# How the first batch's inputs are loaded: chunk by chunk over SyncE and GpSimd, with a new order of all instructions

## The chip, the cores and the metric

The kernel runs on one core of one Trainium2 chip. The metric is the device time of one execution in microseconds (us). Engines are named as the profile names them: PE is TensorE, PEld its weight loads, DVE VectorE, ACT ScalarE, POOL GpSimd, SP SyncE. SP computes nothing here: it issues DMAs on the hardware queue q1. DMAs issued by POOL go to the software queue q0.

## The reference

Two stages, cut to what is computed. Shapes: B, H, S, D = 4, 8, 768, 48, and d_model = H*D = 384.

```python
mag = np.sqrt(a_re * a_re + a_im * a_im)
scale = np.minimum(mag, 0.999) / (mag + 1e-06)
a_re_n, a_im_n = (a_re * scale, a_im * scale)
for t in range(S):
    ar, ai = a_re_n[:, :, t, :, None], a_im_n[:, :, t, :, None]
    S_re, S_im = ar * S_re - ai * S_im + kv(t), ar * S_im + ai * S_re
    y[:, :, t] = q[:, :, t] @ S_re
...
xn = (x - mean) / sqrt(var + 1e-6) * g_ln
out = x + np.maximum(xn @ w_ch1, 0.0) @ w_ch2
```

`kv(t)` is the outer product of k and v at time t. The first stage is a recurrence over time with a complex gate a; `x` is its output with the heads put side by side. All inputs and the output are float32.

## The kernel before, in words

The 768 time steps of each batch are cut into 6 chunks of 128 (24 chunks in all, g = 0 to 23). The chunks stand in groups G0 to G8 (the list `phases`): G0 is chunk 0, G1 chunks 1 and 2, G2 chunks 3 to 5, all of batch 0; G3 is chunks 6 to 8, and so on by threes. G0 and G1 share the first phase.

For each group, `gate_exp` works out the decay of the gate: `ln` of a_re (L411) and its exponential (L414) on ACT, `r` = a_im times that (L393, DVE or POOL by `HOW['r']`), the square of r (`r2`, L393 on DVE or POOL, L397 on ACT), ln(1 + r2) on ACT (L424), their sum and cap on DVE (L427, L434), a cumulative sum over the chunk as a matmul with `u_half` (L440), and two exponentials of it (L445, tile `epn`). A small DMA on SP, `edge`, carries the last row of `epn` (L449). `gate_trig` then needs ACT's other table: arctan of r (L495), sums carried from chunk to chunk (`carry`, L508), the phase by matmuls with `u_turn` (L532 to L536), sine and cosine on ACT (L546) with DVE's passes L543 and L549, the products of q and k with `epn` (`qk`, L584) and of these with sine and cosine (`stk`, L590). ACT's tables are swapped at L372, twice in a phase.

For each chunk, `attention` transposes q and k into `qt` and `kt` (matmuls L617, copies L626; for the later chunks a DMA transpose on SP), forms scores (L642), masks them on DVE (L646), multiplies by v (L668, L670), and carries the state (L711, L713, L718). `feed` is the second stage: moments of x (L734 or L739), its transpose (L750, L754), the first matmul with the folded weight `w1c` (L780), ReLU on ACT or DVE (L786, L788), the second matmul (L801), the residual (L805) and the store on SP (L809). `w1c` is folded at the start from `w1r` and the gains (L310, L320, L324).

Every instruction is added to a plan, and the list `HOW['order']` says in which order they are written out; an engine runs its own in that order and waits where an operand is missing. The strings of `HOW` say which engine takes each operation (V, A, P for DVE, ACT, POOL). `HOW['fill']` gives lengths of filler matmuls on PE ahead of some operations (L169, L173); their results are overwritten.

`HOW['loads']` lists the loads as (what, first, end, engine). "a" is a_re and a_im, "s" is q, k and v; "g", "w1", "w2" are the gains and the thirds of the two weights. a stays float32, the others become bfloat16 on the way. Of batch 0 each array is one tile with all 6 chunks, and `load_fn` has three forms: all six chunks (L213), one chunk (L215), and two chunks that lie three apart (L217, `STEP`): ('a', 1, 3, 'P') loads chunks 1 and 4. By the order, SP issues before its first edge: a_re 0, a_re 3, a_im 0; then edge G0, a_im 3, edge G1. POOL issues: w1 0, a_im 1+4, a_re 1+4, a_re 2+5, a_im 2+5, the gains, (u_half), k 2+5, k 1+4, w1 1, q 0+3, k 0+3, (ident), q 2+5, (u_turn), q 1+4, w1 2, v 1+4, (q of G0, k of G1), v 0+3, (q of G1, k of G0), w2 0, w2 1, (cosine stack of G0), v 2+5, a_re of batch 1, (mask), w2 2, a_im of batch 1, and so on. What stands in brackets is not a load but POOL's work between them: the constants, and the products L584 and L590.

Of the kernel before, what the change touches and what calls it, by code (L numbers as in the profile page):

```python
# [24 lines left out]
STEP = 3  # L25
HOW = {'loads': [('a', 0, 1, 'Y'), ('a', 3, 4, 'Y'), ('a', 1, 3, 'P'), ('a', 2, 4, 'P'), ('g', 0, 0, 'P'),
           ('w1', 0, 0, 'P'), ('w1', 1, 0, 'P'), ('w1', 2, 0, 'P'), ('s', 0, 2, 'P'), ('s', 1, 3, 'P'),
           ('s', 2, 4, 'P'), ('w2', 0, 0, 'P'), ('w2', 1, 0, 'P'), ('w2', 2, 0, 'P'), ('a', 6, 12, 'P'),
# [7 lines left out]
 'r2': 'AVVVVAAAAVVVVVVVVVVVVVVV',  # L36
 'r': 'VVVVVVVVVVPVPPPPPPVPPPPP',
 'carry': 'VVVVPVVVVVPVVVVVPVVVVVPV',
 'st': 'AVVVVVAA',
 'x': 'AAAAAAAVAVVAVAAAVAAAAAAA',  # L40
 'edge': 'YYYYYYYYYYYYYYYYYYYYYYYY',
 'cos': 'VVVVVVVVVVVVVVVVVVVVVVVV',
 'qt': 'AVVVAVVVAVVAAAAAAAAAAAAA',
 'kt': 'AAVAAVVAVVVAVVVVVVVVVVVV',
 'relu': 'AAVVAAAAAAAAAAAVVVAAVAAAAAAVAAVAAAVAAAAVAVAVAVVV',
 'qk': 'PPPPVVPVPVVVVVPPVVVVVVVVVVVVVVVVVVVVVVVVVVVVVVVV',
 'stk': 'VPVVVVVVVVVVVVVVPVVVVVVVVVVVVVVVVVVVVVVVVVVVVVVV',
 'at': 'VVVVVVVVVVVVVVVVVVVVVVVV',
 'xc': 'VAVAAVVAVAVAVVVVVVVVVVVV',
 'xt': 'PPPPPPPPPPPPDDDDDDDDDDDD',  # L50
 'qkt': 'PPPPPPPPPPPPDDDDDDDDDDDD',
 'order': [11, 12, 34, 191, 16, 9, 23, 20, 14, 26, 29, 32, 0, 61, 52, 36, 40, 192, 193, 204, 205, 43, 1, 58, 194, 2,
           206, 195, 207, 196, 208, 4, 209, 178, 49, 197, 198, 210, 199, 38, 201, 200, 211, 55, 212, 202, 183, 213,
           18, 223, 179, 185, 214, 215, 5, 184, 217, 235, 8, 7, 181, 218, 182, 46, 227, 6, 219, 228, 220, 10, 234,
           230, 221, 231, 224, 222, 232, 67, 225, 187, 233, 69, 186, 238, 226, 493, 188, 189, 239, 180, 64, 464, 236,
           240, 470, 190, 465, 243, 241, 73, 242, 244, 471, 237, 245, 3, 487, 71, 246, 462, 488, 485, 80, 463, 510,
           247, 494, 486, 251, 508, 252, 511, 248, 253, 472, 509, 249, 466, 473, 250, 254, 467, 489, 256, 495, 490,
           468, 512, 257, 496, 491, 229, 469, 516, 258, 513, 492, 259, 260, 474, 475, 271, 498, 497, 87, 264, 476,
           514, 261, 499, 479, 515, 265, 502, 518, 267, 520, 263, 477, 266, 262, 521, 503, 480, 522, 268, 478, 94,
           270, 269, 524, 272, 538, 500, 274, 519, 539, 273, 481, 275, 517, 101, 276, 501, 530, 532, 525, 279, 523,  # L60
           504, 278, 277, 533, 280, 531, 281, 555, 482, 553, 534, 505, 556, 526, 282, 506, 554, 283, 535, 284, 576,
           285, 574, 577, 287, 286, 536, 575, 288, 557, 527, 289, 540, 302, 558, 528, 578, 292, 290, 541, 483, 293,
           579, 561, 559, 537, 298, 294, 562, 543, 299, 295, 542, 544, 560, 300, 580, 296, 303, 564, 136, 545, 565,
           297, 581, 304, 584, 301, 547, 108, 566, 306, 305, 602, 548, 603, 563, 594, 307, 596, 595, 604, 585, 617,
           546, 597, 619, 618, 638, 308, 598, 605, 588, 620, 599, 310, 568, 639, 122, 309, 621, 311, 549, 567, 312,
           622, 313, 600, 586, 601, 314, 589, 569, 625, 115, 587, 640, 315, 582, 319, 623, 321, 641, 316, 320, 626,
           607, 317, 642, 583, 624, 570, 318, 608, 322, 324, 335, 643, 609, 325, 550, 627, 326, 327, 551, 610, 606,
           628, 334, 328, 644, 571, 330, 629, 329, 572, 590, 331, 645, 332, 129, 336, 333, 630, 338, 337, 650, 164,
           646, 339, 660, 647, 591, 683, 340, 661, 611, 592, 684, 662, 612, 342, 685, 663, 356, 632, 686, 343, 668,
           664, 631, 648, 613, 341, 633, 357, 669, 651, 665, 344, 358, 687, 670, 688, 359, 345, 704, 666, 652, 671,  # L70
           360, 705, 667, 143, 346, 361, 691, 706, 362, 347, 653, 348, 649, 634, 707, 363, 349, 150, 350, 708, 364,
           614, 673, 365, 674, 709, 654, 367, 689, 366, 655, 368, 635, 370, 351, 656, 353, 672, 352, 690, 369, 354,
           384, 373, 615, 694, 675, 695, 383, 374, 657, 696, 676, 658, 375, 636, 396, 371, 387, 376, 692, 697, 388,
           377, 379, 378, 710, 380, 711, 381, 389, 385, 382, 730, 714, 698, 715, 386, 392, 390, 677, 391, 724, 732,
           678, 393, 790, 731, 716, 733, 699, 791, 394, 745, 712, 395, 718, 397, 751, 400, 679, 398, 764, 401, 399,
           726, 402, 700, 727, 784, 719, 752, 717, 403, 728, 747, 729, 418, 720, 693, 735, 748, 713, 419, 805, 766,
           404, 749, 767, 750, 405, 770, 754, 680, 786, 771, 420, 406, 768, 787, 824, 737, 422, 769, 407, 701, 792,
           421, 774, 793, 807, 738, 788, 157, 408, 681, 423, 756, 702, 409, 789, 808, 811, 757, 795, 739, 721, 826,
           424, 410, 827, 758, 411, 809, 425, 776, 412, 740, 426, 413, 777, 778, 810, 772, 814, 415, 427, 794, 741,
           446, 428, 734, 429, 759, 414, 812, 430, 797, 416, 431, 171, 432, 722, 435, 459, 760, 458, 436, 753, 798,  # L80
           773, 816, 779, 449, 437, 445, 742, 438, 817, 761, 762, 441, 439, 828, 442, 799, 440, 450, 829, 818, 832,
           443, 454, 447, 444, 451, 743, 780, 448, 452, 455, 800, 842, 456, 460, 813, 850, 834, 781, 453, 782, 863,
           848, 836, 849, 457, 851, 801, 830, 819, 835, 837, 882, 831, 844, 461, 820, 845, 433, 869, 902, 821, 846,
           865, 870, 847, 838, 866, 853, 802, 884, 923, 867, 885, 888, 868, 871, 889, 886, 872, 908, 904, 887, 909,
           910, 905, 852, 822, 855, 892, 911, 906, 839, 803, 856, 857, 840, 929, 907, 925, 858, 913, 874, 926, 890,
           942, 891, 896, 927, 897, 859, 928, 912, 875, 876, 860, 931, 894, 861, 877, 932, 930, 915, 895, 944, 916,
           878, 945, 917, 879, 936, 918, 946, 937, 898, 947, 948, 950, 949, 919, 880, 934, 920, 899, 921, 900, 952,
           935, 954, 953, 938, 955, 956, 939, 940, 957, 958],
 'fill': {187: 0.92, 199: 3.58, 219: 1.07, 464: 0.59, 487: 2.58}}


class Plan:

    PIPE = {"V": 0.08, "A": 0.09}

    def __init__(self, rings, slots):
        self.ops, self.makers, self.touch = [], {}, {}
        self.rings, self.slots = rings, slots  # L100
# [24 lines left out]
def kernel(  # L125
# [15 lines left out]
    NCH = S // C  # L141
# [78 lines left out]
    def issue(eng, us, makes, fn, a, pieces, each, got, after=(), hog=False):  # L220
        key = ("dma", len(plan.ops))
        plan.add(ENG[eng], us, (fn, a), [], [key] + makes)
        for i in range(pieces):
            plan.add("Q", each, None, [key], [("moved", len(plan.ops))] + (got if i == pieces - 1 else []),
                     lag=2.0, ring=ENG[eng])

    def load(eng, g0, g1, names, after=()):

        b, c0, c1 = g0 // NCH, g0 % NCH, g0 % NCH + g1 - g0
        us = 0.5 if eng is Y else 0.66 + 0.26 * (c1 - c0)  # L230
        for n in names:
# [642 lines left out]
```

## Time and profile before

| | us |
|---|---|
| median of 3 runs (213.97 to 214.59) | 214.07 |
| the profiled execution, its own time | 214.43 |
| its span, first to last instruction | 212.6 |
| PE busy | 173.3 |
| PEld busy | 135.6 |
| DVE busy | 164.8 |
| ACT busy | 146.3 |
| POOL busy | 102.8 |

The span is the time of the profiled execution without what lies ahead of its first and behind its last instruction. Busy times of engines overlap, so no one of them is the time; what counts is which engine the others wait for in each stretch. Rows of the timeline give the start, the time, the engine, the line, the operation, its output and input, and in square brackets how long the engine stood idle before and what ended that. A row that joins several instructions says how many (x2). DMA rows name the queue, its packets and megabytes in the window asked for, and their time as a share of the 16 DMA engines' time.

### The profile page before, as it was taken

The numbers are of one execution on the slowest core, as the hardware profiler recorded it, in microseconds if no ns is written. First come the engines' busy times: TensorE is split into PE (matmuls) and PEld (weight loads), VectorE is DVE, ScalarE is ACT, GpSimd is POOL, SyncE is SP. The second block draws the span as 40 slices with busy tenths as digits, with TensorE's granted clock in tenths as the row PEclk, the third lists the DMA queues.
The fourth block names the chain that finished last, engine by engine and source line by source line (L and its number), as shares of the span: only waits on it lengthen the run. The fifth ranks groups of instructions, "written<-read, shape, count | busy, mean of one in ns | idle before, by whom it ended". The sixth has DMA issues, their size and how long they took to land.

```text
span 212.6 us, 5419 instructions
## 1 busy us (share of the span) xinstructions
PE 173.3 (82%) x2296; PEld 135.6 (64%) x2296; DVE 164.8 (78%) x262; ACT 146.3 (69%) x205; POOL 102.8 (48%) x89
## 2 busy tenths in 40 slices
PE   0019744979999899998978989987999996999992
PEld 0003314968977688776765857676776765988770
DVE  1018799999999999979899999987987994554351
ACT  4025947499998999988997978967898514453210
POOL 8986798708541476196994010293285820010100
PEclk9999995799999999999999999999999998799999
DMA  6999999994999299999999928969969797752122
GB/s 97 238 184 160 162 134 171 222 240 71 144 119 109 74 75 210 158 161 190 162 71 232 225 92 161 232 144 171 172 65 154 169 192 170 198 120 59 56 77 76
DMA packets 116997, 31.44 MB, mean 148 GB/s; under 512 B 109100, under 2 KB 114956, under 8 KB 116972
## 3 DMA queue, kind: packets, MB, share of 16 engines
q0 software_dynamic: 79104, 18.09, 92.6%
q1 hardware_dynamic: 37868, 13.00, 26.5%
q8 instruction: 18, 0.29, 0.6%
q14 instruction: 7, 0.06, 0.1%
HBM read 28.31 MB, written 4.72 MB: 155 GB/s over the span
## 4 chain that ended last, share of the span: by engine, by line
PE 40%; DVE 22%; DMA 12%; issue 9%; ACT 8%; POOL 5%; SPq 1%; DVEq 0%; POOLq 0%; ACTq 0%
PE h_ps L780 13%; PE o_ps L801 13%; DMA qkt<-stk 8%; DMA ar<-in_a_re_dram 5%; DVE stk L590 4%; PE a_ps L642 3%; DVE w1c L324 3%; PE qk_ps L169 2%; DVE lm L427 2%; ACT epn L445 2%; DVE w L549 2%; PE qk_ps L617 1%; ACT ht L786 1%; DVE o L805 1%; PE l_ps L440 1%
## 5 line engine op out<-in xcount | busy, mean ns | idle before, releaser
L780 PE MATMUL h_ps<-xt,w1c 128*128 128x128 bf16 x864 | 54.6, 221 | 0.2
L780 PEld LDWEIGHTS <-w1c 128*128 128x128 bf16 x864 | 50.7, 99 | 2.4 <-issue 0.6
L801 PE MATMUL o_ps<-w2b,ht 128*128 128x384 bf16 x288 | 50.4, 326 | 0.0
L801 PEld LDWEIGHTS <-ht 128*128 128x128 bf16 x288 | 27.3, 98 | 17.0 <-issue 0.4
L646 DVE TENSOR_TENSOR at<-a_ps,mask 128x1024 bf16<-128x1024 f32 x24 | 29.3, 1219 | 10.0 <-PE a_ps L642 9.7
L786 ACT ACTIVATE ht<-h_ps 128x1024 bf16<-128x1024 f32 (+1 forms) x33 | 26.7, 825 | 11.2 <-PE h_ps L780 11.2
L584 POOL TENSOR_TENSOR epn<-qk,epn 128x1152 bf16<-128x1152 bf16 (+2 forms) x8 | 14.6, 1828 | 17.7 <-ACT epn L445 15.1
L744 POOL TENSOR_SCALAR rs<-mv 128x3 f32<-128x3 f32 x8 | 2.2, 278 | 40.8 <-ACT junk L734 26.2
L445 ACT ACTIVATE epn<-l_ps 128x384 bf16<-128x384 f32 (+1 forms) x32 | 18.6, 652 | 4.7 <-PE l_ps L440 4.6
L805 DVE SCALAR_TENSOR_TENSOR o<-o_ps,rs,x 128x384 f32<-128x384 f32 x24 | 14.4, 610 | 9.5 <-PE o_ps L801 6.5
L642 PE MATMUL a_ps<-qkt 128*128 128x128 bf16 x192 | 15.1, 223 | 3.9 <-DMA qkt<-stk 2.9
L173 PE MATMUL l_ps<-ident 128*128 128x512 bf16 x16 | 5.7, 532 | 15.0 <-POOL ident masks.py:199 15.0
L411 ACT ACTIVATE rec<-ar 128x1152 f32<-128x1152 f32 (+2 forms) x9 | 9.5, 1054 | 11.6 <-DMA ar<-in_a_re_dram 11.6
L393 DVE TENSOR_TENSOR r<-ai,m 128x384 bf16<-128x384 f32 x12 | 6.2, 560 | 14.0 <-DMA ai<-in_a_im_dram 10.9
L372 ACT ACT_TABLE_LOAD x12 | 15.4, 1283 | 0.9 <-PEq L858 0.7
L173 PEld LDWEIGHTS <-ident 128*128 128x128 bf16 x24 | 2.8, 118 | 20.7 <-POOL ident masks.py:199 15.0
L642 PEld LDWEIGHTS <-qkt 128*128 128x128 bf16 x192 | 12.0, 99 | 5.4 <-DMA qkt<-stk 3.2
L788 DVE TENSOR_SCALAR ht<-h_ps 128x512 bf16<-128x512 f32 (+1 forms) x15 | 13.2, 891 | 2.5 <-PE h_ps L780 2.4
L617 PE MATMUL qk_ps<-ident,stk 128*128 128x128 bf16 x192 | 13.6, 223 | 1.6 <-DVE stk L590 1.3
L617 PEld LDWEIGHTS <-stk 128*128 128x128 bf16 x192 | 11.9, 99 | 2.5 <-DVE stk L590 1.5
L424 ACT ACTIVATE m<-lm,one 128x1152 f32<-128x1152 bf16 (+2 forms) x9 | 10.3, 1149 | 4.1 <-DVE lm L393 4.0
L393 POOL TENSOR_TENSOR r<-ai,m 128x384 bf16<-128x384 f32 x12 | 11.6, 994 | 2.9 <-ACT m L414 2.8
(106 smaller groups left out, 388.4 us busy)
## 6 DMA issues: line engine op xcount, KB each, us to landing
out_dram<-o SPq DMA_DIRECT2D x24, 192.0 KB, 3.9
ar<-in_a_re_dram POOLq DMA_DIRECT2D x3, 1152.0 KB, 10.3
ai<-in_a_im_dram POOLq DMA_DIRECT2D x3, 1152.0 KB, 12.0
qk<-in_q_dram POOLq DMA_DIRECT2D x3, 576.0 KB, 9.9
qk<-in_k_dram POOLq DMA_DIRECT2D x3, 576.0 KB, 9.9
v<-in_v_dram POOLq DMA_DIRECT2D x3, 576.0 KB, 8.4
w1r<-in_moe_w_ch_dram POOLq DMA_DIRECT2D x3, 384.0 KB, 10.3
w2b<-in_moe_w_ch_dram POOLq DMA_DIRECT2D x3, 384.0 KB, 7.2
```

The costliest lines, as they stand in the source:

```text
L372: op(A, 1.28, old, [key], lambda: A.preload_act_table_set(TABLES[which]))
L393: times = lambda eng, out, x, y: eng.tensor_tensor(out=out, in0=x, in1=y, op=ALU.mult)
L445: A.activation(out=o, in_=banks(G["l_ps", j], m), func=AF.Exp, scale=(1.0, -1.0)[s])
L584: eng.tensor_tensor(out=o, in0=part(G, "qk"[s]).rearrange("p h c d -> p c h d"), in1=i, op=ALU.mult)
L617: T.transpose(ps[:, h], G["stk"][:, int(which == "ks"), j, ts(h, C)], K["ident"])
L642: T.matmul(ch["a"][:, h], lhsT=ch["kt"][:, h], rhs=ch["qt"][:, h], start=True, stop=True)
L646: V.tensor_tensor(out=ch["at"], in0=ch["a"], in1=K["mask"].unsqueeze(1).to_broadcast([C, H, C]), op=ALU.mult)
L780: T.matmul(ps[:, jj], lhsT=w1c[:, i, ts(j0 + jj, C)], rhs=ch["xt"][:, i], start=(i == 0), stop=(i == ND - 1))
L786: A.activation(out=o, in_=i, func=AF.Relu)
L788: V.tensor_scalar(out=o, in0=i, scalar1=0.0, scalar2=None, op0=ALU.max)
L801: T.matmul(ps, lhsT=ch["ht"][:, i], rhs=w2b[:, i], start=(i == 0), stop=(i == NJ - 1))
L805: V.scalar_tensor_tensor(out=ch["o"], in0=ch["o_ps"], scalar=stats[u, "rs"][:, ds(j, 1)], in1=ch["x"], op0=ALU.mult, op1=ALU.add)
```

## The change

The loads of batch 0 and the engines and order of all operations change; the operations themselves do not.

- a of batch 0: all six chunks one by one on SP (12 DMAs), none on POOL. In the new order SP issues a_re 2, a_re 0, a_im 0, a_re 1, a_im 2, a_im 1, a_re 3, a_re 4, then edge G0, a_re 5, a_im 5, a_im 3, a_im 4, then edge G1.
- q and k of batch 0: chunk by chunk on POOL (12 DMAs where there were 6 of two chunks); v of batch 0: one DMA of all six chunks where there were 3.
- POOL's new order at the start: w1 0, gains, w1 1, r2 of G0, q 0, k 0, q 1, w1 2, (ident, u_half), k 1, k 2, q 2, (u_turn), w2 0, (k and q of G0, sine stack of G0), v whole, k 5, q 4, k 4, q 3, (mask), w2 2, q 5, a_re of batch 1, k 3, (a carry of G2), w2 1, a_im of batch 1, and so on.
- Batches 1 to 3 are loaded whole on POOL, as before. The two-chunk form of `load_fn` gives way to a general one that no load of the new list uses.
- Engines: r2 of G0 goes from ACT to POOL and that of G2 from DVE to ACT; of 48 ReLU passes DVE has 11 (15 before); of 24 copies of qt and kt DVE has 6 and 20 (8 and 18); of the products with q and k POOL has 6 (8), of those with sine and cosine 1 (2).
- The filler before matmuls: 2.67, 0.26, 0.81 and 2.49 us where it was 0.92, 3.58, 1.07, 0.59 and 2.58.

```diff
-STEP = 3
-HOW = {'loads': [('a', 0, 1, 'Y'), ('a', 3, 4, 'Y'), ('a', 1, 3, 'P'), ('a', 2, 4, 'P'), ('g', 0, 0, 'P'),
-           ('w1', 0, 0, 'P'), ('w1', 1, 0, 'P'), ('w1', 2, 0, 'P'), ('s', 0, 2, 'P'), ('s', 1, 3, 'P'),
-           ('s', 2, 4, 'P'), ('w2', 0, 0, 'P'), ('w2', 1, 0, 'P'), ('w2', 2, 0, 'P'), ('a', 6, 12, 'P'),
+HOW = {'loads': [('a', 0, 1, 'Y'), ('a', 1, 2, 'Y'), ('a', 2, 3, 'Y'), ('a', 3, 4, 'Y'), ('a', 4, 5, 'Y'), ('a', 5, 6, 'Y'),
+           ('g', 0, 0, 'P'), ('w1', 0, 0, 'P'), ('w1', 1, 0, 'P'), ('w1', 2, 0, 'P'), ('qk', 0, 1, 'P'),
+           ('qk', 1, 2, 'P'), ('qk', 2, 3, 'P'), ('qk', 3, 4, 'P'), ('qk', 4, 5, 'P'), ('qk', 5, 6, 'P'),
+           ('v', 0, 6, 'P'), ('w2', 0, 0, 'P'), ('w2', 1, 0, 'P'), ('w2', 2, 0, 'P'), ('a', 6, 12, 'P'),
            ('s', 6, 12, 'P'), ('a', 12, 18, 'P'), ('s', 12, 18, 'P'), ('a', 18, 24, 'P'), ('s', 18, 24, 'P')],
...
- 'r2': 'AVVVVAAAAVVVVVVVVVVVVVVV',
+ 'r2': 'PVAVVAAAAVVVVVVVVVVVVVVV',
...
- 'relu': 'AAVVAAAAAAAAAAAVVVAAVAAAAAAVAAVAAAVAAAAVAVAVAVVV',
- 'qk': 'PPPPVVPVPVVVVVPPVVVVVVVVVVVVVVVVVVVVVVVVVVVVVVVV',
- 'stk': 'VPVVVVVVVVVVVVVVPVVVVVVVVVVVVVVVVVVVVVVVVVVVVVVV',
+ 'relu': 'AAAVVVAAAAAVAVAAAVAAVAAAAAAAAVVVAAAAAAAAAAVAAAAA',
+ 'qk': 'PPVVVVPVPPVPVVVVVVVVVVVVVVVVVVVVVVVVVVVVVVVVVVVV',
+ 'stk': 'PVVVVVVVVVVVVVVVVVVVVVVVVVVVVVVVVVVVVVVVVVVVVVVV',
...
- 'fill': {187: 0.92, 199: 3.58, 219: 1.07, 464: 0.59, 487: 2.58}}
+ 'fill': {227: 2.67, 256: 0.26, 470: 0.81, 493: 2.49}}
...
-            eng.dma_start(out=inp[n, b].rearrange("p h c d -> p (h c) d")[:, c0::STEP],
-                          in_=view.rearrange("p h c d -> p (h c) d")[:, c0::STEP])
+            eng.dma_start(out=inp[n, b][:, :, c0:c1], in_=view[:, :, c0:c1])
...
-                  1.0, [("got_" + n, b, c) for c in (range(c0, NCH, STEP) if c1 - c0 == 2 else range(c0, c1))])
+                  1.0, [("got_" + n, b, c) for c in range(c0, c1)])
```

The list `order` is replaced as a whole, and the strings r, carry, x, qt, kt and xc change in some places.

## What the change does to the time: the prediction

> **What bounds the kernel now.** The page was read first. The profiled execution took 214.43 us around a span of 212.6, so 1.8 us lie outside; the median of the three timed runs is 214.07, 0.2% less. By the busy rows TensorE has 82% and VectorE 78% of the span. The busy time by stretches says where: four stages with different limits.
>
> ```profile
> 0.00:17.50 17.50, 2.51 (x6) 0.89 (x7) 2.55 (x10) 5.04 (x7) 15.00 (x23) 1.00 1.37 170
> 17.50:45.00 27.50, 19.51 (x166) 13.11 (x165) 25.15 (x48) 17.88 (x23) 20.06 (x17) 0.88 1.71 178
> 45.00:100.00 55.00, 51.07 (x762) 41.87 (x762) 52.61 (x81) 50.77 (x71) 28.59 (x17) 1.00 1.42 136
> ...
> 180.00:212.60 32.60, 28.47 (x378) 23.31 (x376) 13.20 (x18) 9.61 (x20) 2.09 (x4) 0.95 0.37 102
> ```
>
> The columns after the length are PE, PEld, DVE, ACT, POOL. Up to 17.5 us only POOL works, and it issues loads. Then DVE is full (25.2 of 27.5, later 52.6 of 55), and the end is TensorE's. So what starts DVE sooner moves everything behind it, unless a later stage has a limit of its own.
>
> What DVE waits for is in the timeline of the first 25 us:
>
> ```profile
> 12.73 0.56 DVE L393 TENSOR_TENSOR r<-ai,m 128x384 bf16<-128x384 f32 x1 [10.92 <-DMA ai<-in_a_im_dram]
> ...
> 14.62 0.84 ACT L411 ACTIVATE rec<-ar 128x768 f32<-128x768 f32 x1 [9.99 <-DMA ar<-in_a_re_dram]
> ...
> 16.37 1.13 DVE L393 TENSOR_TENSOR r<-ai,m 128x384 bf16<-128x384 f32 x2 [3.08 <-ACT m L414]
> ...
> 24.77 1.26 ACT L495 ACTIVATE r<-r 128x384 bf16<-128x384 bf16 x2
> ...
> 44.97 1.23 DVE L646 TENSOR_TENSOR at<-a_ps,mask 128x1024 bf16<-128x1024 f32 x1
> ```
>
> Chunk 0's a_im, issued on SP at 1.85, is used at 12.73; a_re of chunks 1 and 2, issued on POOL with chunks 4 and 5, at 14.62. The first masked scores (L646) come at 44.97. Why so late is in the DMA queues' packets (packets, MB, share of 16 engines), here for 2 to 3, 6 to 7, 10 to 11 and 26 to 28 us:
>
> ```profile
> q1 hardware_dynamic: 986, 0.19, 99.3%
> ...
> q0 software_dynamic: 142, 0.14, 80.6%
> q1 hardware_dynamic: 422, 0.08, 42.2%
> ...
> q0 software_dynamic: 67, 0.21, 101.8%
> q1 hardware_dynamic: 11, 0.00, 1.8%
> ...
> q0 software_dynamic: 647, 0.21, 89.6%
> q1 hardware_dynamic: 599, 0.12, 51.8%
> ```
>
> q1 is SP's queue, q0 POOL's. A chunk of one array is 1024 packets on q1 (0.19 MB of 192 bytes). Alone, SP moves 986 in a microsecond; beside POOL's fp32 loads of a (0.21 MB in 67 packets) it moves 11. So a_im of chunk 0 crawled behind loads that nobody needed yet.
>
> **The change part by part.**
>
> *a over SP.* POOL loses four two-chunk loads and SP gets eight more single ones, twelve in all. SP's issues took 0.42 to 0.81 us, mean 0.56; eight stand before the first edge DMA, 4.5 us on a queue that otherwise waits until 21.74 for that edge. POOL's loads in this time are now w1 0, the gains, w1 1, and then r2 of group 0, which waits. Packets: before, q1 had moved 48, 986 and 889 by 4 us, 1923. While w1 0 moved (388 packets, 3 to 7 us) q1 moved 117, 29 and 422, so 568. w1 1 follows at once; I take 568 again, which gives 3059 at 10 us. Chunk 0's a_im is the third on SP and ends with packet 3072; with the 0.5 us that a_re took from its last packet (by 3.0) to its use, r of group 0 starts at 10.5. Bounds: 8.6 if q1 keeps 532 a microsecond, as at 7 to 8; 11 if it keeps 29. From there SP is alone at 986: a_re 1 at 11.5, a_im 2 at 12.6, a_im 1 at 13.6. ln and its exponential (0.84 each) end at 13.2, the last r of group 1 at 14.4, against 17.52: 3.1 us sooner (2.0 to 4.7).
>
> The Trainium skill, "DMA: Bandwidth & Descriptors", section "Issuing engines are not separate DMA queues", says the opposite of such a gain: DMAs of all issuers interleave on the same engines, and another issuer saves only the issuing time. By that the sum would be no more than POOL's issue time below; the row of 11 packets against 986 speaks against it here. The same page's "Anatomy of one DMA" puts a fixed 2.0 us on each DMA of GpSimd's path, an estimate of 24 us for twelve chunks if they were served singly; the queue's rows (986 packets, then 889 across two loads) show no gap, and the sum takes none.
>
> *q, k by chunk, v whole.* POOL loses the four loads of a (1.16, 1.16, 1.16, 1.19), six of q and k (7.0) and three of v (3.6): 15.3 us of issue. It gets v whole (2.3) and twelve single chunks, which no row shows. From 1.16 for two chunks and 2.25 for six, one costs about 0.9; bounds 0.75 (a weight's load) and 1.16. Net -2.2 us, between -4.0 and +0.9. In order: r2 of group 0 ends at about 12.0 (0.9 like POOL's 384 products; it was 0.51 on ACT), then three chunks, w1 2, ident and u_half (0.5 each), three chunks, u_turn: 19.7. Before, u_turn was done at 16.6. w2 0 to 20.5, two products to 22.4, one stack product (1.65, after sin at 22.9) to 24.5, v to 26.8, four chunks to 30.4, the mask by 32.1. The last of q and k for group 1 is issued by 19.2. Their landings took 10 us before behind a full queue and 2.8 on an empty one; I take 4, since nine loads are no longer ahead. At 10, DVE's product at about 22 would stand 6 us.
>
> *The chain to arctan.* From 14.4: r2 0.56, ln 0.93, both 0.94, cap 0.36, cumulative sum 0.5, two exponentials 1.5, table 1.28, so arctan starts at about 20.6 (24.77 before) and its first is done at 21.4.
>
> *DVE's list.* Before, from 17.54 to 44.97 its list holds 26.9 us by its rows: it is the limit. The new one, from r2 of group 1 to the first mask, is 23.1 by rows without collisions: qt 1, qt 2 and kt 2 (0.7 each) go elsewhere or later, r2 of group 2 (0.76) goes to ACT, the product of 2.24 to POOL; two products of 0.56, one of 0.54 and kt 1 (0.7) come in. Up to 3 us more if POOL's operations beside it slow it, as the 2.24 for 128x768 beside 0.95 for twice that show, and 1.71 for a carry. Its 6.4 us ahead of arctan fit into the wait for it; 16.7 to 19.7 follow from 21.7: first mask at 38.4 to 41.5. The third mask ended at 49.85, 4.9 after the first one's start; it is 6.1 now, since kt 2 and a product stand between: 44.6 to 47.6, with that product (0.75) done ahead. So 3 to 6 us sooner; I take 4.5.
>
> *Later.* Batch 1's loads are unchanged and POOL reaches them no later. ReLU passes go from 15 to 11 on DVE and 33 to 37 on ACT, all of them in the second half of the chunks, where ACT has slack (9.6 busy in the last 32.6 us). I cost that at nothing; it is worth some 2 us of DVE, and if DVE's cover were gone in the tail, four passes of 0.57 to 1.02 on ACT cost up to 4. TensorE's filler is 2.5 us less, all in its early waits: nothing.
>
> 214.43 - 4.5 = 209.9; against the median that is 209.6, and I say **209.8**.
>
> **The rivals.**
>
> *Issue time alone.* The loads keep DVE waiting as before and POOL's queue gives 2.2 us at most a part of which reaches DVE: about 213. For it: DMA is full from 5 to 48 us, and total bytes are the same. Against: the order of bytes changes, and 11 packets a microsecond is no fair share.
>
> *The last four chunks of a starve on SP (slower).* a_re 5, a_im 5, a_im 3 and a_im 4 stand behind the edge of group 0, so they start at about 17 to 18. Their 4096 packets compete with POOL's cast loads (300 a microsecond by the last fence), w2 0 (29 to 190), and v. DVE's three r of group 2 stand ahead of the stack products of group 1, so all behind them waits. In my sum 600 packets pass by 20.5, few beside w2 0, and 986 a microsecond pass between 23 and 26 while POOL is held by its products; the rest end at 27.5, and r is due at 28. If POOL's queue is not held there, all go at 240 to 300: 13.7 to 17 us, plus 2.5 beside w2 0, so 34 to 38. r of group 2 ended at 38.3 before, and from there 6.6 us of the new list remain. From a landing at 38 on, the kernel is slower; at 40 it is 2 us slower, about 216.5; beside fp32 loads of batch 1 it would be far worse. Against: those come only after 33 us.
>
> *More than that.* If SP holds 532 a microsecond beside w1, DVE sees no collisions and the 2 us of ReLU reach the end: 4.7 + 1.5 + 2 gives about 206.
>
> **How the numbers follow.** Forecast 45% (own range 208 to 211.5), more than that 10%, issue time alone 13%, starving 32%. Less than 0.3% (0.6 us) can't be told from no change. The forecast and the large gain are faster, and about 5 of the 13 points of issue time; 8 points are the same; starving is slower: 0.60, 0.08, 0.32. Below 205.5 I leave 6%, and above 217.5 some 13%, where DVE waits for these chunks or for q and k too.
>
> **What would show it.** SP's twelve loads stand in a row from 0.7 us, and q1 has about 986 packets a microsecond once w1 1 is through. r of group 0 starts near 10.5, the second table load near 19.3 (23.47 now), the first mask at 38 to 41. The forecast is wrong if DVE idles for a DMA of a_im of the second group, or stands at its own products for q and k, or if the first mask comes sooner and the span does not follow, which would be a limit in the 45 to 180 us that I have not seen.

## The result, and the profile after

The changed kernel takes 208.66 us (median of 4 runs, 205.94 to 209.94), beside 214.33 (213.97 to 215.0) for the kernel before on the same chip. The ratio is 0.965, with a 95% interval of 0.956 to 0.973: **faster, by 2.7 to 4.4%**. A second taking of the same kernel on another occasion gave 208.42 (206.29 to 209.41) and a ratio of 0.979 (0.969 to 0.988), so a gain of 1.2 to 3.1%. The ratios leave disturbed runs out, so they are not the quotients of the medians. The profiled execution took 209.94, the slowest of the four, around a span of 208.1, which is 4.5 us less than the span of before (212.6). In the lines below the line numbers are two less than those of before: L391 is its L393 (r), L409 its L411, L493 its L495, L644 its L646.

First the busy time by the same stretches. The columns after the length are PE, PEld, DVE, ACT, POOL, then the granted clock of PE, the DMA share and GB/s:

```profile
0.00:17.50 17.50, 1.78 (x4) 0.62 (x5) 5.76 (x26) 5.72 (x8) 9.86 (x18) 1.00 1.18 164
17.50:45.00 27.50, 22.77 (x230) 15.95 (x230) 23.09 (x39) 23.51 (x34) 18.91 (x21) 0.88 1.61 162
...
180.00:208.10 28.10, 24.39 (x317) 19.31 (x314) 7.57 (x10) 11.56 (x25) 2.09 (x4) 1.00 0.32 83
```

In the first stretch DVE does 5.76 us of work where it did 2.55, and POOL 9.86 where it did 15.00. In the last one the whole picture is 4.5 us shorter. The DMA bandwidth of the first two stretches did not rise (164 and 162 GB/s; 170 and 178 before): the same queues do not move more, they move other things first.

What starts the work, and two later rows, in the timeline of DVE and ACT (start, us, engine, line, operation, idle time before and what ended it):

```profile
9.52 0.56 DVE L391 TENSOR_TENSOR r<-ai,m 128x384 bf16<-128x384 f32 x1 [8.12 <-DMA ai<-in_a_im_dram]
...
11.79 0.84 ACT L409 ACTIVATE rec<-ar 128x768 f32<-128x768 f32 x1 [3.02 <-DMA ar<-in_a_re_dram]
...
13.54 1.03 DVE L391 TENSOR_TENSOR r<-ai,m 128x384 bf16<-128x384 f32 x2 [2.48 <-ACT m L412]
...
21.40 1.26 ACT L493 ACTIVATE r<-r 128x768 bf16<-128x768 bf16 x2
...
30.51 1.49 DVE L391 TENSOR_TENSOR r<-ai,m 128x384 bf16<-128x384 f32 x3
...
38.60 1.23 DVE L644 TENSOR_TENSOR at<-a_ps,mask 128x1024 bf16<-128x1024 f32 x1
...
56.93 1.50 DVE L391 TENSOR_TENSOR r<-ai,m 128x384 bf16<-128x384 f32 x3 [0.83 <-DMA ai<-in_a_im_dram]
...
60.67 1.14 DVE L803 SCALAR_TENSOR_TENSOR o<-o_ps,rs,x 128x384 f32<-128x384 f32 x2 [1.46 <-POOL rs L743]
```

Chunk 0's r starts at 9.52 (12.73 before), ln of chunks 1 and 2 at 11.79 (14.62), arctan at 21.40 (24.77), the first mask at 38.60 (44.97). The first three come 2.8 to 3.4 us sooner, which is the loads; between arctan and the first mask another 3.0 are gained. The r of chunks 3 to 5, at 30.51, have no bracket: DVE did not stand for the four loads of a that come last on SP.

The queues in the same microseconds as before (packets, MB, share of 16 engines): 2 to 3, 6 to 7, 10 to 11, and two microseconds, 26 to 28.

```profile
q1 hardware_dynamic: 977, 0.19, 96.1%
...
q0 software_dynamic: 129, 0.10, 63.6%
q1 hardware_dynamic: 618, 0.12, 60.7%
...
q1 hardware_dynamic: 1200, 0.23, 114.2%
q0 software_dynamic: 18, 0.01, 8.1%
...
q1 hardware_dynamic: 826, 0.15, 37.9%
```

Between 10 and 11 us q1 carries 1200 packets of needed a where it had 11. By 28 us it has nothing left to move.

POOL's own timeline shows why q0 is empty at 10 us, and also the one thing that went against the forecast:

```profile
10.16 0.82 POOL L391 TENSOR_TENSOR lm<-r 128x384 bf16<-128x384 bf16 x1 [6.44 <-DVE edge L277]
10.94 0.96 POOL L215 DMA_DIRECT2D qk<-in_q_dram  x1
...
43.68 0.91 POOL L506 TENSOR_TENSOR carry<-carry,r 128x384 bf16<-128x384 bf16 x1 [5.85 <-DVE carry L506]
...
45.33 2.26 POOL L213 DMA_DIRECT2D ai<-in_a_im_dram  x1
47.56 2.23 POOL L213 DMA_DIRECT2D qk<-in_q_dram  x1
57.18 2.22 POOL L213 DMA_DIRECT2D qk<-in_k_dram  x1 [7.39 <-issue]
59.48 0.19 POOL L742 TENSOR_SCALAR rs<-mv 128x3 f32<-128x3 f32 x1
```

The same two operations of POOL before, a_im of batch 1 and the first chunk's rs:

```profile
39.14 2.25 POOL L213 DMA_DIRECT2D ai<-in_a_im_dram  x1
...
54.20 0.82 POOL L744 TENSOR_SCALAR rs<-mv 128x3 f32<-128x3 f32 x1
```

r2 of group 0 stands 6.44 us for its operand, and no load of q and k is issued before 10.94. (The profile puts the wait down to DVE's fill of `edge`, which stands right behind that r in its list; what r2 needs is the r that starts at 9.52.) Later POOL stands 5.85 us at a carry, issues a_im of batch 1 at 45.33 (39.14 before), then stands 7.39 ahead of k of batch 1, and comes to the first chunk's rs only at 59.48 (54.20 before). DVE pays for both, in the last two rows of its timeline: 0.83 us for a_im, 1.46 for rs. A third loss carries no bracket. One pass of DVE between the two masks takes 0.92 us longer, first before, then after:

```profile
54.21 0.76 DVE L543 TENSOR_SCALAR fr<-w 128x1152 int16<-128x1152 int16 x1
```

```profile
48.70 1.68 DVE L541 TENSOR_SCALAR fr<-w 128x1152 int16<-128x1152 int16 x1
```

It now begins while POOL issues q of batch 1 (47.56 to 49.79) and ends 0.59 us after that issue; before, it met no issue. So of 5.1 us that the start had gained by the third mask (43.51; 48.63 before), 2.2 were left at chunk 3's mask (63.49; 65.69). At chunk 12's (129.24; 133.52) it was 4.3, at chunk 23's (188.27; 193.67) 5.4.

### The profile page after: what moved, and what is told of

Read it like the earlier page. It is cut to its first block, busy times and chain, and to the rows that moved or that the text cites. A ratio compares the mean times of both kernels' runs of the same rounds, so it can differ in the third digit from the quotient of the medians.

```text
span 208.1 us, 5401 instructions
## 1 busy us (share of the span) xinstructions
PE 172.7 (83%) x2287; PEld 134.8 (65%) x2287; DVE 158.3 (76%) x258; ACT 150.6 (72%) x211; POOL 95.0 (46%) x87
## 3 DMA queue, kind: packets, MB, share of 16 engines
q1 hardware_dynamic: 46188, 14.57, 32.0%
## 4 chain that ended last, share of the span: by engine, by line
PE 37%; DVE 17%; issue 13%; POOL 11%; DMA 10%; ACT 6%; SPq 4%; POOLq 0%; ACTq 0%; DVEq 0%
PE o_ps L799 12%; PE h_ps L778 11%; DMA ar<-in_a_re_dram 4%; POOL qk L213 4%; DVE stk L588 3%; DMA xt<-x 3%; DMA qkt<-stk 3%; DVE w L547 3%; PE qk_ps L169 2%; DVE at L644 2%; POOL ai L213 2%; SPq L628 2%; PE a_ps L640 2%; PE qk_ps L615 2%; PE th_ps L173 2%
## 5 line engine op out<-in xcount | busy, mean ns | idle before, releaser
L784 ACT ACTIVATE ht<-h_ps 128x1024 bf16<-128x1024 f32 (+1 forms) x37 | 29.7, 821 | 14.9 <-PE h_ps L778 14.9
L644 DVE TENSOR_TENSOR at<-a_ps,mask 128x1024 bf16<-128x1024 f32 x24 | 29.2, 1220 | 6.4 <-PE a_ps L640 5.9
L742 POOL TENSOR_SCALAR rs<-mv 128x3 f32<-128x3 f32 x8 | 3.6, 450 | 52.0 <-ACT junk L732 33.4
L803 DVE SCALAR_TENSOR_TENSOR o<-o_ps,rs,x 128x384 f32<-128x384 f32 x24 | 14.4, 611 | 14.3 <-PE o_ps L799 10.3
L391 POOL TENSOR_TENSOR r<-ai,m 128x384 bf16<-128x384 f32 x12 | 11.7, 999 | 16.5 <-ACT m L412 16.5
L318 PE MATMUL w_ps<-w1r,centre 128*128 128x512 bf16 x9 | 3.6, 527 | 16.2 <-DVE centre L308 15.4
L409 ACT ACTIVATE rec<-ar 128x1152 f32<-128x1152 f32 (+2 forms) x9 | 9.5, 1055 | 8.8 <-DMA ar<-in_a_re_dram 8.7
L716 DVE TENSOR_TENSOR s<-t_ps,dec 128x384 bf16<-128x384 f32 x20 | 11.0, 551 | 6.2 <-PE t_ps L711 5.9
L391 DVE TENSOR_TENSOR r<-ai,m 128x384 bf16<-128x384 f32 x12 | 6.3, 562 | 11.4 <-DMA ai<-in_a_im_dram 9.0
L615 PEld LDWEIGHTS <-stk 128*128 128x128 bf16 x192 | 11.3, 98 | 4.6 <-DVE stk L588 1.7
L666 PE MATMUL y_ps<-v,at 128*128 128x48 bf16 x192 | 12.4, 184 | 2.2 <-DVE at L644 2.2
L582 POOL TENSOR_TENSOR epn<-qk,epn 128x1152 bf16<-128x1152 bf16 (+1 forms) x6 | 11.2, 1879 | 4.2 <-ACT epn L443 4.2
L666 PEld LDWEIGHTS <-at 128*128 128x128 bf16 x192 | 10.8, 96 | 3.5 <-DVE at L644 2.7
## 6 DMA issues: line engine op xcount, KB each, us to landing
ar<-in_a_re_dram POOLq DMA_DIRECT2D x3, 1152.0 KB, 10.5
```

The source lines that it names most:

```text
L391: times = lambda eng, out, x, y: eng.tensor_tensor(out=out, in0=x, in1=y, op=ALU.mult)
L615: T.transpose(ps[:, h], G["stk"][:, int(which == "ks"), j, ts(h, C)], K["ident"])
L644: V.tensor_tensor(out=ch["at"], in0=ch["a"], in1=K["mask"].unsqueeze(1).to_broadcast([C, H, C]), op=ALU.mult)
L666: T.matmul(hd(ps)[:, h], lhsT=ch["at"][:, h], rhs=vt[:, h, c], start=True, stop=sp is None)
L784: A.activation(out=o, in_=i, func=AF.Relu)
L803: V.scalar_tensor_tensor(out=ch["o"], in0=ch["o_ps"], scalar=stats[u, "rs"][:, ds(j, 1)], in1=ch["x"], op0=ALU.mult, op1=ALU.add)
```

## The experiments

The question was which part of the change made the start sooner, since it has four: a on a queue of its own, the sequence of its chunks, POOL's hold at r2, and DVE's new list. Then whether the later loss can be mended, and what the start is still worth. The kernels are built from the changed one, except the sixth. Their line numbers are those of before, but for the changed kernel's second taking; those of the sixth are three higher. "SP" and "POOL" in the diffs below stand for that engine's part of the list `order`, with the loads named by chunk.

| kernel | us, median | range | ratio to before | 95% interval |
|---|---|---|---|---|
| 1. changed kernel again | 208.42 | 206.29 to 209.41 | 0.979 | 0.969 to 0.988 |
| 2. r2 of G0 on ACT | 212.79 | 211.37 to 213.72 | 1.003 | 0.998 to 1.008 |
| 3. k of batch 1 behind rs | 208.24 | 206.67 to 209.75 | 0.983 | 0.974 to 0.991 |
| 4. SP in the old sequence | 215.7 | 213.22 to 215.93 | 1.015 | 1.004 to 1.025 |
| 5. a on POOL | 211.2 | 208.81 to 213.19 | 0.989 | 0.981 to 0.998 |
| 6. new loads, old order | 216.35 | 212.98 to 217.18 | none given | |
| 7. rs and a_im of batch 1 early | 205.74 | 203.61 to 207.94 | 0.970 | 0.963 to 0.977 |
| 8. ReLU engines of before | 207.08 | 204.28 to 207.88 | 0.980 | 0.965 to 0.994 |
| 9. a alone ahead | 205.53 | 204.27 to 208.0 | 0.968 | 0.962 to 0.974 |
| 10. 7 and 9 together | 204.2 | 202.54 to 205.75 | 0.966 | 0.951 to 0.980 |
| 11. as 10, other order of loads | 204.35 | 202.91 to 206.7 | 0.968 | 0.959 to 0.976 |

They ran on four chips: 1 to 4 on one, 5, 6, 7 and 9 on the next, 8 and 10 on the third, 11 on the fourth. The kernel before took 213.72, 213.58, 212.83 and 213.63 there, so across chips the ratio compares better than the median. The interval of the ratio of 1 overlaps with those of 3, 5 and 7 to 11; it does not with those of 2 and 4.

The profiles of experiments 5, 6 and 11 are, like that of the changed kernel, executions at the upper end of their kernel's range; what is read from them are rows of the start and waits for loads there.

### 1. The changed kernel again

No edit.

> The changed kernel as it is, once more, beside the kernel before. Expected: a ratio near 0.965 to 0.975, first mask at 38 to 39 us, rs of the first unit near 59.5 us.

208.42 us, and a ratio of 0.979, a smaller gain than was expected. Its profiled execution starts arctan at 21.75 and the first mask at 39.70, has the third mask at 44.66 and chunk 3's at 63.84, with rs at 59.15. So the first mask of one kernel moves by 1.1 us from one execution to another, and a difference of that size in one profile proves nothing. The loss between the third mask and chunk 3's is there again (19.2 us; 20.0 in the first profile, 17.1 before), though r of group 3 does not wait for a_im here: DVE stands 1.06 us for rs, and the long pass takes 1.41.

### 2. Without POOL's hold: r2 of group 0 on ACT

```diff
- 'r2': 'PVAVVAAAAVVVVVVVVVVVVVVV',
+ 'r2': 'AVAVVAAAAVVVVVVVVVVVVVVV',
```

> The changed kernel, but r2 of G0 on ACT, so that POOL does not stand before its loads of q and k. Theory (SP must be alone while a comes): q and k start near 4 us, share the DMA engines packet by packet with a, SP falls from about 1000 to 300 to 550 packets a microsecond after 9 us; the last r of group 1 ends 2 to 4 us later than 14.6, arctan starts 1 to 3 us later than 21.4, ratio 0.975 to 0.985. Rival (the hold does not matter, the gain is the order of bytes on SP): r of group 1 ends within 1 us of 14.6, POOL's constants and products come some 5 us earlier, ratio at or below 0.965.

Nothing but one square of 128x384 moves. POOL, with nothing to wait for, issues q of chunk 0 at 3.72 instead of 10.94. Between 10 and 14 us the queues carry this, and DVE's r of the last chunk of group 1 comes late:

```profile
q0 software_dynamic: 2690, 0.27, 119.6%
q1 hardware_dynamic: 1496, 0.28, 64.8%
```

```profile
19.27 0.56 DVE L393 TENSOR_TENSOR r<-ai,m 128x384 bf16<-128x384 f32 x1 [3.31 <-DMA ai<-in_a_im_dram]
```

The changed kernel's q1 carried 3554 packets in these four microseconds, and 4213 in its second taking. Here it is 1496, since POOL's bf16 loads of q and k take their turns beside it. Arctan starts at 26.64, the first mask at 43.66, and the whole gain is gone: 212.79, by the medians 4.4 us more than the changed kernel (by the ratios 5). **The theory was right in kind and too low in size: the wait of r2, 6.4 us of an idle engine, is worth some 4.4 us of the kernel's time.** It acts as a gate that keeps POOL's loads back until a_im of chunk 0 has landed.

### 3. k of batch 1 behind rs

```diff
  POOL:
- a_im 6-11, q 6-11, k 6-11, rs 0
+ a_im 6-11, q 6-11, rs 0, k 6-11
```

> The changed kernel with POOL's load of k of batch 1 behind rs of the first unit, not ahead of it. Theory (POOL's wait of 7.4 us before that load holds rs, the first residuals and what is behind them on DVE, and eats part of the gain): rs starts at 50 instead of 59.5 us, the first mask of chunk 3 comes 1 to 3 us before 63.5, span 1 to 2.5 us shorter. Rival (a_im of batch 1, landed at 56.9, sets the end of this stage): rs at 50, mask of chunk 3 within 0.5 us of 63.5, same time.

rs starts at 50.16 instead of 59.15, and the stage from the third mask to chunk 3's takes 19.1 us as before the edit (43.80 to 62.91). r of group 3 is at 57.07, behind a wait of 0.68 for a_im of batch 1. 208.24: no change. The time is as the rival said; the mask of chunk 3, at 62.91, lies between the two. The wait for rs was real, but a_im stands right behind it, and the pass of 1.68 us is still there.

### 4. SP's twelve loads in the old sequence

```diff
  SP:
- a_re 2, a_re 0, a_im 0, a_re 1, a_im 2, a_im 1, a_re 3, a_re 4, edge G0, a_re 5, a_im 5, a_im 3, a_im 4
+ a_re 0, a_re 3, a_im 0, a_im 1, a_im 4, a_re 1, a_re 4, a_re 2, a_re 5, a_im 2, a_im 5, a_im 3, edge G0
```

> The changed kernel with SP's twelve loads in the old kernel's sequence of chunks (a_re 0, a_re 3, a_im 0, a_im 1 and 4, a_re 1 and 4, a_re 2 and 5, a_im 2 and 5, a_im 3), all ahead of the first edge. Theory (bytes that are needed first must come first): a_im 0 as before, a_re 2 is now the eighth and a_im 2 the tenth load, so r of group 1 ends at 17 to 19 us instead of 14.6, arctan starts 2 to 4 us later, first mask at 40.5 to 42.5, ratio 0.975 to 0.985. Rival (only the queue matters, or DVE's shorter list): first mask within 1 us of 38.6, ratio as the changed kernel.

All a is on SP, chunk by chunk, and POOL still holds; only what comes first differs (and edge G0, which comes behind all twelve).

```profile
22.45 1.03 DVE L393 TENSOR_TENSOR r<-ai,m 128x384 bf16<-128x384 f32 x2 [10.25 <-DMA ai<-in_a_im_dram]
```

a_im of chunk 2 lies tenth. From 10 to 12 us q1 moves 1056 and 1111 packets a microsecond; it then shares with q and k (1096 packets beside 889 from 14 to 16 us, 915 beside 1651 from 16 to 18). First mask 47.73, time 215.7: slower than before (ratio 1.004 to 1.025). The direction was expected and the size was not. Four chunks more ahead of the last needed one (it is tenth, it was sixth) cost 8.9 us (22.45 against 13.57), 2.2 each and not the 1 us that a chunk takes alone: POOL's hold ends at about 11 us, and the rest of the list falls into the crowd. What the later edge adds was not tried apart.

### 5. a on POOL's queue, in the same order

```diff
- ('a', 0, 1, 'Y'), ('a', 1, 2, 'Y'), ('a', 2, 3, 'Y'), ('a', 3, 4, 'Y'), ('a', 4, 5, 'Y'), ('a', 5, 6, 'Y'),
+ ('a', 0, 1, 'P'), ('a', 1, 2, 'P'), ('a', 2, 3, 'P'), ('a', 3, 4, 'P'), ('a', 4, 5, 'P'), ('a', 5, 6, 'P'),
```

> The changed kernel with all twelve loads of a on POOL, each at its place in the order; the chunks come in the same sequence, on one queue with w1. Theory (what counts is that nothing unneeded is ahead of or beside the bytes that are needed): POOL issues 12 loads at 0.9 us, a_im 1 is issued at about 11 and r2 of G0 stands behind; q0 moves 0.2 MB a microsecond, so r of group 1 ends at 13.5 to 16 (14.6 in the changed kernel), but the last four chunks of a and POOL's loads of q, k and v come 2 to 6 us later, first mask at 39.5 to 43, ratio 0.975 to 0.995. Rival (SP's own queue is the gain): as slow as the kernel before or slower, r of group 1 at 17 or later.

The queues between 10 and 14 us, first of this kernel, then of the changed one in its second taking:

```profile
q0 software_dynamic: 378, 0.97, 104.2%
```

```profile
q1 hardware_dynamic: 4213, 0.80, 100.3%
q0 software_dynamic: 36, 0.01, 2.6%
```

POOL's queue moves 0.97 MB, SP's 0.80: the issuer gives no bandwidth of its own. Yet r of group 0 comes at 12.56 (10.47 in that taking), r of group 1 ends at 16.23, just behind the expected range, arctan at 24.10, the first mask at 42.50, and the time is 211.2, 2.8 us more by the medians. By the ratios it is some 2 us, and the two intervals overlap (0.981 to 0.998, 0.969 to 0.988). Twelve issues at 0.9 us on an engine that also computes are 10.8 us of POOL; that this is what SP's queue saves is argued, not shown.

### 6. The new loads in the order and on the engines of before

```diff
  the kernel before: only its loads and load_fn; SP's list as in the changed kernel,
  POOL's new loads where its old ones stood
- ('a', 0, 1, 'Y'), ('a', 3, 4, 'Y'), ('a', 1, 3, 'P'), ('a', 2, 4, 'P'), ...
+ ('a', 0, 1, 'Y'), ('a', 1, 2, 'Y'), ('a', 2, 3, 'Y'), ('a', 3, 4, 'Y'), ('a', 4, 5, 'Y'), ('a', 5, 6, 'Y'), ...
```

> The kernel before, its order and engines, with only the new loads put where the old ones stood: a chunk by chunk on SP in the new sequence, q and k by chunk and v whole on POOL, and no operation that holds POOL ahead of q and k. Theory (the hold and the order are half of it): q and k run beside a as in the run with r2 on ACT, r of group 1 ends at 17 to 20, first mask at 43.5 to 47, ratio 0.99 to 1.02. Rival (the loads alone make the gain): r of group 1 ends at 14 to 15, first mask at 41 to 42, ratio 0.975 to 0.985.

```profile
17.86 1.03 DVE L396 TENSOR_TENSOR r<-ai,m 128x384 bf16<-128x384 f32 x2 [6.17 <-DMA ai<-in_a_im_dram]
```

The two r of group 1 end at 18.89 (17.50 before), arctan is at 25.98, the first mask at 46.70; 216.35 beside 213.58, with 212.98 as the lowest run and no interval that settles the sign. Between 10 and 14 us q1 has 1690 packets and q0 2133, a crowd like that of experiment 2. **The loads by themselves gain nothing at the start.**

### 7. rs and a_im of batch 1 early

```diff
  POOL:
- k 3, carry G2, w2 1, a_im 6-11, q 6-11, k 6-11, rs 0
+ k 3, w2 1, a_im 6-11, carry G2, q 6-11, rs 0, k 6-11
```

> As the run with rs ahead of k of batch 1, and w2 1 and a_im of batch 1 also ahead of the carry that holds POOL for 5.8 us. Theory (the stage from the third mask to the mask of chunk 3 takes 19 to 20 us instead of 17.1 because a_im of batch 1 lands at 57): r of group 3 does not wait, starts at 55.5 to 56.5, mask of chunk 3 at 61 to 62.3, time 0.5 to 1.5 us under the changed kernel. Rival (DVE, ACT and PE are full there anyway, the stage is longer because of what the list holds): mask of chunk 3 within 0.6 us of 62.9, same time.

```profile
56.56 1.49 DVE L393 TENSOR_TENSOR r<-ai,m 128x384 bf16<-128x384 f32 x3
```

No bracket: the wait for a_im is gone, and rs is at 50.15. The edit does a third thing: q of batch 1 is issued from 47.04 to 49.29, so the long pass of DVE no longer meets it.

```profile
49.94 0.75 DVE L543 TENSOR_SCALAR fr<-w 128x1152 int16<-128x1152 int16 x1
```

The stage takes 17.6 us (third mask 44.57, chunk 3's 62.18), nearly what it took before the change (17.1). r of group 3 comes only 0.5 us sooner than in the third experiment, because this execution's third mask is 0.8 later. 205.74: 2.7 us below the changed kernel by the medians, some 2 by the ratios, whose intervals just overlap. In the profiles 1.4 of it are there at chunk 17's mask (142.17; 143.59 in the second taking); the rest lies in the tail, of which the last section tells. The wait for rs alone was worth nothing (experiment 3). a_im alone was not tried, but in experiments 1, 2, 4, 5 and 8 r of group 3 does not wait for a_im and the stage still takes 19.2 to 20.1 us.

### 8. The ReLU passes as before, chunks 12 to 23

```diff
- 'relu': 'AAAVVVAAAAAVAVAAAVAAVAAAAAAAAVVVAAAAAAAAAAVAAAAA',
+ 'relu': 'AAAVVVAAAAAVAVAAAVAAVAAAAAAVAAVAAAVAAAAVAVAVAVVV',
```

> The changed kernel with the engines of the ReLU passes of chunks 12 to 23 as before (9 of 24 on DVE, where the changed kernel has 4). Theory (that move is worth nothing or little, since DVE has slack in the last third): mask of chunk 17 within 1 us of 143.4, time within 1 us of the changed kernel's 208.4. Rival (it is worth 2 us or more): time 2 us or more above it.

In this half nine of 24 passes are DVE's again, where the changed kernel has four. 207.08, against 208.42 with the moved passes: the ranges overlap and the ratios (0.980 and 0.979) are the same. Moving the five passes from DVE to ACT shows no worth; the interval (0.965 to 0.994) could hide 2 us.

### 9. a alone ahead: both w1 loads behind POOL's hold too

```diff
  POOL:
- w1 0, gains, w1 1, r2 of G0, q 0, k 0, q 1, w1 2, ident, u_half, k 1, k 2, q 2, u_turn, w2 0
+ gains, u_half, ident, u_turn, r2 of G0, q 0, k 0, w1 1, q 1, k 1, k 2, q 2, w1 0, w1 2, w2 0
  PE:
- w_ps 1, l_ps of G0, l_ps of G1
+ l_ps of G0, l_ps of G1, w_ps 1
```

> The changed kernel with POOL's hold made complete: w1 0 and w1 1 go behind r2 of G0 too, the constants u_half, ident and u_turn ahead of it, and PE does the first two cumulative sums ahead of its first product with w1. Theory: SP is alone from the start, so a_im 0 (packet 3072) lands near 5.5, a_im 1 (6144) near 8.7; r of group 1 ends at 9.5 to 10.5 instead of 14.6, arctan starts at 16 to 18 instead of 21.4, first mask 2 to 5 us earlier, time 2 to 4.5 us under the changed kernel, ratio 0.95 to 0.965. Rival (DVE's list or w1 is the limit behind it): r of group 1 as said, but DVE waits for w1 or for q and k, and the first mask is within 1 us of 38.6 to 39.7.

l_ps is the cumulative sum, w_ps the product of w1. r of group 0 starts at 5.98, now waiting for the exponential and not for a load; arctan at 16.80. 205.53. But DVE then stands for the product of w1, whose load was put back:

```profile
17.22 0.75 DVE L324 SCALAR_TENSOR_TENSOR w1c<-w1r,gln,w_ps 128x512 bf16<-128x512 bf16 x1 [3.98 <-PE w_ps L320]
```

Of the 5.0 us that arctan came sooner (21.75 in the second taking), 3.0 are left at the first mask (36.71).

### 10. Experiments 7 and 9 together, with w1c behind the phase

```diff
  POOL: as in 9, and from k 3 on as in 7
  PE, DVE:
- w_ps 1, w1c 1.1, w1c 1.0, ..., th_ps of G1, quarter of G1
+ th_ps of G1, w_ps 1, ..., quarter of G1, w1c 1.1, w1c 1.0
```

> The two edits that gained, together: w1 behind r2 of G0 with a alone at the start, and a_im of batch 1 and rs ahead of POOL's waits; and PE's first product with w1 goes behind the phase matmuls, so that neither these nor DVE's carry wait for w1 as in the run with a alone. Theory: arctan at 16.8 as there, first mask at 35 to 36.5 (36.7 there), mask of chunk 3 at 58 to 60 (61.5 and 62.2), mask of chunk 17 at 138.5 to 140.5, median 203 to 205, ratio 0.95 to 0.96. Rival (the gains do not add, a later stage takes them back): mask of chunk 17 at 141 or later, median 205.5 or more.

```profile
19.34 1.67 DVE L584 TENSOR_TENSOR epn<-qk,epn 128x768 bf16<-128x768 bf16 x1 [1.03 <-DMA qk<-in_k_dram]
...
25.41 2.06 DVE L324 SCALAR_TENSOR_TENSOR w1c<-w1r,gln,w_ps 128x512 bf16<-128x512 bf16 x3 [1.29 <-PE w_ps L320]
...
31.16 1.03 DVE L393 TENSOR_TENSOR r<-ai,m 128x384 bf16<-128x384 f32 x2 [1.09 <-DMA ai<-in_a_im_dram]
```

204.2, the lowest median of all, but a ratio of 0.966, like 7 alone (0.970) and 9 alone (0.968). The first mask was expected at 35 to 36.5 and came at 38.83, chunk 3's at 58 to 60 and came at 61.16, chunk 17's at 138.5 to 140.5 and came at 141.08: these parts missed, and that the two gains add is not shown. The 3.98 us went, but what had been behind it (k of chunk 0, w_ps, a_im of group 2) took 3.4 of them.

### 11. As 10, with k ahead of q and w1 sooner

```diff
  POOL, behind r2 of G0:
- q 0, k 0, w1 1, q 1, k 1, k 2, q 2, w1 0, w1 2, w2 0
+ w1 1, k 0, q 0, k 1, k 2, w1 0, q 1, q 2, w1 2, w2 0
```

> As the run with both parts (a alone ahead on SP, rs and a_im of batch 1 early), with POOL's loads behind r2 in the order w1.1, k of chunk 0, q of chunk 0, k of 1, k of 2, w1.0, q of 1, q of 2, w1.2, w2.0. Theory (VectorE stood 1.0 us for k of chunk 0 and 1.3 us for the product of w1, because they were issued behind q and w1.0): both waits are gone or under 0.3 us, the first mask starts at 36.0 to 37.5 (38.83 there), and the median is 202.5 to 204. Rival (the start is held by something else, TensorE's clock or the next DMA in the list): the waits move to w1.0 or to q of chunks 1 and 2, the first mask stays at 38.3 or later, and the median is 204 or more.

The product with k waits no more and is at 18.30, and takes 0.55 us instead of 1.67. w_ps still costs 1.01, a_im of group 2 now 1.65. 204.35: the same. The profiled execution is its slowest (206.7; the mean granted clock was 0.963), so its first mask at 40.49 isn't set against the others; by the median the rival held.

## Why the prediction was right, and where it was off

**Start of the queue.** It said that SP would not be alone at 986 packets until 10 us and that r of group 0 would start at 10.5 (8.6 to 11). It was 9.52 and, again, 10.47. The last r of group 1 was to end at 14.4 and ended at 14.57. Two errors cancelled here, which is luck. q1 had moved 3830 packets by 10 us (3706 in the second taking) where the sum had 3059. But r did not start 0.5 us after packet 3072: that count was passed at about 7.7 us (8.1), and r started 1.8 us later (2.4). What held the last packets of that load was not looked into. Arctan was to start at about 20.6 and started at 21.40 and 21.75.

**What the gain hangs on.** The sum had the hold in it ("then r2 of group 0, which waits", "From there SP is alone"), but as a part of POOL's schedule, without a price of its own. Experiment 2 prices it at 4.4 us, as much as the whole forecast of 4.5. The heading of that part, *a over SP*, named the wrong edit as the cause: the loads in the old order gain nothing (6), and with a bad sequence they lose (4). Sequence, hold and own queue are worth 7.3, 4.4 and 2.8 us by the medians, each taken away alone; the last is not clear of noise, and the first has the later edge in it. They add up to far more than the gain of 5.7, as they would if each needed the others; no run takes two away at once.

**The rule of the Trainium skill.** "DMA: Bandwidth & Descriptors", section "Issuing engines are not separate DMA queues", was weighed against the 11 packets beside 986. Experiment 5 agrees with the page on bandwidth (0.97 MB on q0 alone, 0.80 on q1 alone, in four microseconds) and so do the stretches, whose GB/s did not rise. The prediction said that the row "speaks against it"; it doesn't. The row shows unneeded bytes that take nearly all of the same engines' time (101.8% beside 1.8%) while needed ones wait, and the rule says nothing of which bytes go first. By the rule alone SP's queue is worth what it saves of POOL's issuing; measured, that is 2.8 us by the medians, with intervals that overlap. The fixed 2.0 us for each DMA, from "Anatomy of one DMA" on the same page, was rightly left out of the sum: on SP the loads went through at 977 to 1200 packets a microsecond in the rows above in which its queue was alone, and on POOL's own path, 0.97 MB in 4 us leaves no room for such gaps.

**q, k and v.** One chunk was to take 0.9 us of POOL, bounds 0.75 and 1.16; it takes 0.87 to 0.96. u_turn was to be done at 19.7 and is at 19.6, the mask by 32.1 and it is there at 32.15. q and k of groups 0 and 1 landed 3.9 to 5.5 us after their issue, where 4 was taken; DVE's products did not stand for them.

**DVE's list.** From the start of arctan to that of the third mask it took 23.86 us before and 24.39 in experiment 6, which has the old list; with the new one it took 22.11 and 22.91 in the changed kernel and 21.92 in experiment 2. So 1 to 2 us go with the new list and not with a load. Part of that may be TensorE's clock, which fell in both profiles of the old list there (last section). The first mask was to start at 38.4 to 41.5 and started at 38.60 and 39.70. The third ended at 44.73 and 45.88, within 44.6 to 47.6: a gain of 5.1 and 4.0, where 4.5 was taken out of 3 to 6.

**The rivals.** *The last four chunks of a* did not starve: q1 had 826 packets between 26 and 28 and r at 30.51 did not wait. In the faster starts of 9 and 10 that rival shows its face: r of group 2 waits 0.2 to 1.1 us for a_im. *Issue time alone* fell with the first mask. *More than that* counted on SP's 532 beside w1, which q1 held only from 6 to 8 us (618 and 538; 168 from 8 to 9), and on the 2 us of ReLU, which experiment 8 does not show.

**The step that failed** is the first sentence of *Later*: "Batch 1's loads are unchanged and POOL reaches them no later." POOL reaches a_im of batch 1 6.2 us later, behind w2 1 and a carry that DVE is late with, and rs 5.3 us later. Nor did the prediction ask what POOL's issues would meet on a DVE that is 5 us ahead: that of q of batch 1 now meets the long pass. Between the third mask and chunk 3's 2.9 us were lost, and the rows hold 0.83 for a_im, 1.46 for rs and 0.92 for the pass. Experiment 7 removed all three, and the stage took 17.6 us; which of them counts for how much was not tried apart. The ReLU passes, too, were told wrongly: 15 to 11 is nine to four in the second half of the chunks and six to seven in the first. The 2 us that the large-gain rival gave them were not seen in experiment 8.

**Why it came out near 209.8 all the same.** The gain at chunk 23's mask was 5.4 us, more than the 5.1 of the start, so the later stages gave back what chunk 3 had lost. Which of the many edits to the order did that was not tried, so that the end came out near the forecast is in part luck. In the profiled execution the tail spent some of it: from chunk 17's mask to the end it took 65.0 us, against 64.2 before, and that differs between executions, as told below.

## What to carry to other kernels

Under a full DMA queue the order of bytes is the schedule: ask of every transfer that runs before the first needed one lands whether it could be issued later, and hold it back by placing it behind an operation that waits for that landing, even if the issuing engine then stands idle for 6 us. Price such a hold by taking it away, since it looks like waste in a profile. When a start moves, follow the engine that issues the next batch's loads: one instruction on it that waits for the busy engine moves all loads behind it, and a wait that is removed alone may only uncover the next. Look, too, for operations that merely grew longer: they carry no wait in a profile.

## What the runs showed of the hardware

**Packets don't share evenly.** Two queues at once gave 11 packets of 192 bytes beside 67 of POOL's fp32 ones (before, 10 to 11 us), 1496 beside 2690 of POOL's packets for bf16 loads (experiment 2, 10 to 14 us), and 977 to 1200 a microsecond on SP's queue alone. "DMA: Bandwidth & Descriptors", section "Queues, rings and completion order", of the Trainium skill has an engine take the queues in turn, packet by packet; equal numbers in these rows would have fitted it, and the rows of this case don't have them, as far as the profile's packets are the page's.

**POOL can stand before a DMA that needs nothing.** Ahead of k of batch 1 it stood 7.39, 5.91, 7.13 and 7.20 us (the changed kernel twice, experiments 2 and 9), with no operand missing. In the twelve profiles other than that of the kernel before, k was issued 0.3 to 0.4 us after a_im of that batch had landed: 57.18 after 56.83 in the changed kernel, and 55.06 after 54.75 in experiment 7, where a_im took 15.2 us to land and POOL stood 2.35. In the kernel before a_im had landed before POOL came to k, and it did not stand. So this wait follows the landing of the whole-batch load two places ahead; why was not isolated.

**A pass of DVE can wait out POOL's issue of a DMA.** The long pass (`fr`, 128x1152) took 0.75 to 0.76 us in the four profiles in which it meets no issue (before, experiments 7, 10 and 11). In the other nine it took 1.08 to 1.68 and ended 0.55 to 0.59 us after the issue that it met. The product of q with `epn` just ahead of it in the changed kernel (two inputs, 0.75 us at 48.03) ran inside the same issue and grew by nothing.

**TensorE's clock dips, in some executions.** Busy time and clock (the first number behind POOL's count) in five microseconds, of the kernel before and of the changed one:

```profile
180.00:185.00 5.00, 5.00 (x81) 4.77 (x80) 2.21 (x3) 1.38 (x3) 0.00 (x0) 0.70 0.81 208
```

```profile
175.00:180.00 5.00, 4.45 (x65) 4.28 (x66) 2.40 (x4) 1.38 (x4) 0.00 (x0) 0.66 0.81 198
```

The clock falls to about two thirds for some microseconds. In experiment 7 it is 1.00 there. The six profiles without a dip behind chunk 17's mask (experiments 4 and 7 to 11) take 60.9 to 61.9 us from that mask to the end, the seven with one 63.0 to 65.0, the kernel before among them (64.2). So part of what the medians of 7 to 11 gained may be the clock's; how often each kernel dips was not counted. Most profiles have a dip between 20 and 45 us too (lowest five microseconds 0.54 before, 0.50 in the changed kernel and in experiment 6, none in experiments 2, 3 and 8). Each of the seven late dips comes at the end of a wait of TensorE for a DMA of `qkt` or `xt`, of 1.04 to 2.07 us (1.29 before, 1.69 in the changed kernel). But waits of up to 1.54 us have none behind them (experiment 10), so what sets a dip off stays open.
